# Side work of the first layer queued behind the PReLU of the iteration ahead, and two small products moved apart

## The chip, the cores and the metric

The kernel runs on one core of one Trainium2 chip. A core has five engines with an instruction queue each: TensorE (PE, matrix products; its weight loads are shown as PEld), VectorE (DVE), ScalarE (ACT), GpSimd (POOL) and SyncE (SP, which issues DMAs here). Each engine works through its own queue in order, and an instruction that waits for another engine holds up all that is behind it in its queue. The metric is the device time of one execution in microseconds (us); lower is better.

## The reference, cut to what matters

Three stages follow each other on 4608 tokens (8 batches of 576):

```python
def sm_attn(qq, kk, vv):
    s = scale * np.matmul(qq, kk.transpose(0, 1, 3, 2))
    a = np.exp(s - np.max(s, axis=-1, keepdims=True))
    return np.matmul(a / (np.sum(a, axis=-1, keepdims=True) + 1e-09), vv)
p_packed = sm_attn(p, k, v)                # 32 packed rows per head, 8 heads of 64
x = sm_attn(q, p_packed, p_packed)         # -> 4608 x 512
h = x @ w_in                               # first layer, 512 -> 2048
g = np.maximum(h, 0.0) + alpha * np.minimum(h, 0.0)     # PReLU
x = g @ w_out                              # 2048 -> 512
gate, val = x @ w_gate, x @ w_val          # second layer, 512 -> 1536
out = (gate / (1 + np.exp(-gate)) * val) @ w_out2
```

The weights come in double precision, as pairs of 32-bit words, and are narrowed on the chip; products are done in three passes (low x high, high x high, high x low) to keep float32's precision.

## The kernel before, in words

**The first layer** is a loop over 256 iterations (`it`). One iteration is one block of 128 hidden columns (`f`, 16 blocks) for one half batch of 288 tokens (`j`). `h_unit(it)` makes six products into one of two PSUM banks named `h`; then ScalarE writes `m` (alpha times h, L1003), VectorE makes the PReLU `g` from bank and `m` (L1006), ScalarE rounds it to `hi` (L1014), and GpSimd subtracts to `lo` (L1016). The bank is free for `h_unit(it + 2)` when `g` is done. `o_unit(it)` makes twelve products of `hi`, `lo` and `w_out` into the four accumulators, and stands three iterations behind `h_unit` (`LAG1 = 3`). The products with `w_in` are folded: per batch, `ppw` (`pp_win`) holds the packed attention rows times `w_in`, and `h` is made from the softmax `a2` and `ppw`.

**Beside these products** runs other work, traced in `steps(it, 0)` ahead of `h_unit(it)` and in `steps(it, 1)` behind it, so that an iteration has two slots. For batches 2 to 7 the table `STEPS` says in which slot (counted from the start of the batch ahead, 64 slots a batch) each piece of the attention of the next batch stands: loads (`k0`, `q0`, `v0`), transposes on VectorE (`kt0`, `qt0`, L614), logits (`s1a`), maximum, exponential and sums, `et0`/`et1` (transposed exponentials, L678 and L685), `pp0`/`pp1` (their products with `v`, L694, evicted at L702), `ppt`, `s2a`/`s2b`, and the second softmax (`top`, `sub`, `sum`, `mul`, `turn`, `rest`, L730 to L753). `v0` and `v1` share one buffer, so the load of `v1` waits for `pp0`. `PPW` sets the slots of `pp_win` (products L564, evictions L784 and L786). From slot 84 on (`GROUP0`) each slot also issues up to two pieces of the second layer's weight work (`more_weights2`): narrowing (`widen`, L217 to L265), differences (L927), splits into high and low (L933, L934, L944, L945) and stores to DRAM. Up to iteration 37 a table `EARLY` does the same for batches 0 and 1 and the first layer's weights (`pp_win` there evicts at L799 and L800).

**What sets the order.** The program is traced in this order, and a scheduler then lays every engine's queue by a model of the time: an instruction may stand ahead of ones traced earlier when the scheduler takes it to be ready sooner. `tc.issue_after(x)` holds it: what is traced inside the block stands behind `x` if both are on one engine. From iteration 36 on (`CHAIN0`) the products on TensorE are chained so with `behind()` and `done()`, and their queue is in the order traced. The queues of VectorE, ScalarE, GpSimd and SyncE are free, but for four conversions held by `HOLD`.

**The second layer** is a loop over 6 x 12 steps without side work from the first, apart from its own inputs (`ring` tiles, made in the last 36 iterations of the first layer by `prepare_x`).

Of the kernel before, what the change touches and what calls it, by code (L numbers as in the profile page):

```python
# [11 lines left out]
AF = mybir.ActivationFunctionType  # L12
# [60 lines left out]

STEPS = """
    8:p,k0,k1 10:pt 11:kt0,k2 12:kt1,k3,v0 14:kt2 15:kt3 17:s1a 19:s1b 20:mx0,q0,q1 21:mx1,exp0
    22:exp1 23:sums 24:et0 26:et1 28:qt0,q2,pp0,v1 29:qt1,q3 33:pp1 34:qt2 35:qt3 36:ppt 40:s2a
    42:s2b 44:top0 45:top1 46:sub0 47:sub1 49:sum0 50:sum1 51:mul0 52:mul1 53:turn0 54:turn1
    57:rest0 58:rest1
"""
# [10 lines left out]
GROUP0 = 84  # L90
# [14 lines left out]
def f32(ap):  # L105
    return ap.bitcast(F32)
# [3 lines left out]
def tile_kernel(  # L110
# [23 lines left out]
    nc = tc.nc  # L134
# [71 lines left out]
        return ap if len(other.shape) == 2 else ap.rearrange("p (c f) -> p c f", c=KC)  # L206

    raws, vals, queue, issued = [], [], [], []
    begun = {}

    def use(*cut):
        raws[:] = sum((r for r, _ in cut), [])
# [89 lines left out]
    def mm3(o, wts, xs, start, stop, **kw):  # L302
        whi, wlo = wts
        xhi, xlo = xs
        nc.tensor.matmul(o, wlo, xhi, start=start, stop=False, **kw)  # L305
        nc.tensor.matmul(o, whi, xhi, start=False, stop=False, **kw)  # L306
        return nc.tensor.matmul(o, whi, xlo, start=False, stop=stop, **kw)  # L307
# [239 lines left out]
    before, chained = [], []  # L547

    def behind():

        return tc.issue_after(before[-1].ins) if before else ExitStack()

    def done(last):
        if chained:
            before[:] = [last]
# [308 lines left out]
    plan = {}  # L864
# [14 lines left out]
    busy = set()  # L879
# [3 lines left out]
    for b in range(2, B):  # L883
        d0 = 2 * NB1 * (b - 1)
        steps_of = attention(b)
        for entry in STEPS.split():
            d, names = entry.split(":")
            slot = d0 + int(d)
# [73 lines left out]
    def more_weights2(vector):  # L962

        for _ in range(2):
            if not kinds:
                kinds.append(next(work2, None))
            if kinds[0] is None or kinds[0] == "v" and not vector:
                return
            vector = vector and kinds[0] == "p"
            kinds[:] = [next(work2, None)]  # L970
# [12 lines left out]
    def h_unit(it):  # L983
        j, f, _, _ = order[it]
        b, half = divmod(j, 2)
        w = ppw[b, f // WP]
        c = slice((f % WP) * P, (f % WP + 1) * P)
        tok = slice(half * HS, (half + 1) * HS)
        hp = ps.tile([P, 512], F32, tag="h", name=f"h{it}", bufs=2)[:, :HS]
        with behind():  # L990
            for q2 in range(NQ):
                hi, lo = a2[b, q2]
                last = mm3(
                    hp,
                    (w[:, q2, c], w[:, NQ + q2, c]),
                    (hi[:, tok], lo[:, tok]),
                    q2 == 0,
                    q2 == NQ - 1,
                )
        done(last)  # L1000
        g32 = gp.tile([P, HS], F32, tag="g32", name=f"g32_{it}", bufs=2)
        m = gp.tile([P, HS], F32, tag="r", name=f"m_{it}", bufs=2)
        begun[it] = nc.scalar.activation(  # L1003
            out=m, in_=hp, func=AF.Copy, scale=sal[:, f : f + 1]
        )
        nc.vector.scalar_tensor_tensor(  # L1006
            out=g32, in0=hp, scalar=sg[:, f : f + 1], in1=m, op0=ALU.mult, op1=ALU.max
        )
        gs[it] = split(gp, g32, it, LAG1 + 1, LAG1)

    def split(pool, x, n, bufs, bufs_lo):

        hi = pool.tile(list(x.shape), F32R, tag="hi", name=f"hi{n}", bufs=bufs)
        nc.scalar.activation(out=hi, in_=x, func=AF.Copy)  # L1014
        lo = pool.tile(list(x.shape), F32R, tag="lo", name=f"lo{n}", bufs=bufs_lo)
        nc.gpsimd.tensor_tensor(out=lo, in0=x, in1=f32(hi), op=ALU.subtract)  # L1016
        return hi, lo
# [266 lines left out]


    def steps(it, late):
        for s in plan.get((it, late), ()):
            s()
        slot = 2 * it + late
        if slot >= GROUP0:  # L1290
            more_weights2(slot not in busy)

    due = []
    for it in range(N1 + LAG1):
        if it == CHAIN0:
            chained.append(it)
        steps(it, 0)
        if it < N1:
            h_unit(it)
        steps(it, 1)  # L1300
        due.extend(range(max(it - LAG1, 0), it - LAG1 + 1))

        if it < N1 and len(due) == 1 and order[due[0]][2]:
            continue
        while due:
            o_unit(due.pop(0))
# [44 lines left out]
```

## Time and profile before

| what | value |
|---|---|
| median of 3 runs | 1750.45 us (1748.5 to 1750.59) |
| the profiled execution, its own time | 1752.87 us |
| its span, first to last instruction | 1751.1 us |
| TensorE busy | 1625.2 us (93%) |
| VectorE / ScalarE / GpSimd busy | 947.2 / 686.5 / 798.0 us |
| mean granted TensorE clock | 0.97 |

The page of the profile gives busy shares over the whole span; the stages differ, so the trace is read by stretches. A wait row tells which engine sat idle, until what, how long in total, how often, and the longest. In a timeline an idle time before an instruction stands in brackets with what ended it.

### The profile page before, as it was taken

How to read it: one execution, taken by the hardware profiler on the slowest of the kernel's cores; microseconds unless marked ns; L12 is line 12 of the kernel's file. 1: busy time of each engine (PE TensorE's matmuls, PEld its weight loads, DVE VectorE, ACT ScalarE, POOL GpSimd, SP SyncE). 2: the span in 40 equal slices, each digit the busy share in tenths (PEclk: the TensorE clock that was granted, in tenths of full speed). 3: DMA queues.
4: the chain of work that ended last, by engine and by line, in shares of the span. 5: the costliest groups of instructions: out<-in, count | busy, mean ns of one | idle time of the engine just before them, and what ended most of it. 6: DMA issues, size and time to landing. Idle time of an engine off the chain costs nothing.

```text
span 1751.1 us, 28573 instructions
## 1 busy us (share of the span) xinstructions
PE 1625.2 (93%) x10708; PEld 1468.7 (84%) x10708; DVE 947.2 (54%) x1621; ACT 686.5 (39%) x1512; POOL 798.0 (46%) x824
## 2 busy tenths in 40 slices
PE   5689789999989998999999999989999999999997
PEld 3468687878878887988999989979988998999996
DVE  6999857576675757455343363363354336335332
ACT  6775544545454454544431232232222223223221
POOL 3567755656655465423333343343333334333342
PEclk8899899999999999999999999999999999999999
DMA  9434365654555445332264464445455446445442
GB/s 227 127 98 122 114 178 153 159 151 138 151 138 152 109 139 149 79 78 81 95 245 150 166 204 163 169 163 203 169 182 185 159 148 220 167 146 186 169 169 78
DMA packets 227370, 266.11 MB, mean 152 GB/s; under 512 B 130464, under 2 KB 189856, under 8 KB 227232
## 3 DMA queue, kind: packets, MB, share of 16 engines
q1 hardware_dynamic: 227232, 264.30, 47.7%
q8 instruction: 84, 1.38, 0.3%
q14 instruction: 54, 0.44, 0.1%
HBM read 214.70 MB, written 49.55 MB: 151 GB/s over the span
## 4 chain that ended last, share of the span: by engine, by line
PE 60%; DVE 12%; DMA 9%; issue 7%; POOL 6%; ACT 3%; SPq 2%; POOLq 0%; DVEq 0%; ACTq 0%
PE o L306 5%; PE o L307 5%; PE o L305 5%; PE yb L305 4%; PE yb L307 4%; PE yb L306 4%; PE acc L1029 3%; PE acc L1030 3%; PE acc L1035 3%; DMA wgvd<-cva 3%; PE vb L306 3%; PE vb L307 3%; PE vb L305 3%; PE xb L306 3%; PE xb L307 3%
## 5 line engine op out<-in xcount | busy, mean ns | idle before, releaser
L1016 POOL TENSOR_TENSOR lo<-g,hi 128x288 fp32r<-128x288 f32 x256 | 223.8, 876 | 229.1 <-ACT hi L1014 191.8
L1223 POOL TENSOR_TENSOR s<-s,p 128x384 f32<-128x384 f32 x72 | 73.6, 1023 | 465.7 <-ACT s L1222 465.7
L1006 DVE SCALAR_TENSOR_TENSOR g<-h,sg,m 128x288 f32<-128x288 f32 x256 | 129.9, 509 | 165.8 <-ACT m L1003 145.2
L305 PE MATMUL h<-a2h,ppw 128*128 128x288 f32 x512 | 165.5, 323 | 53.8 <-DVE g L1006 46.7
L1184 DVE TENSOR_TENSOR u<-vb,u 128x384 f32<-128x384 f32 x144 | 80.2, 557 | 186.5 <-PE vb L307 186.4
L1014 ACT ACTIVATE hi<-g 128x288 fp32r<-128x288 f32 x256 | 112.7, 441 | 158.6 <-DVE g L1006 150.2
L305 PEld LDWEIGHTS h<-a2h,ppw 128*128 128x128 f32 x512 | 99.4, 194 | 89.5 <-DVE g L1006 60.8
L307 PE MATMUL o<-wp,ph 128*128 128x512 f32 x432 | 172.2, 399 | 0.0
L306 PE MATMUL o<-wp,ph 128*128 128x512 f32 x432 | 171.6, 397 | 0.0
L305 PE MATMUL o<-wp,pl 128*128 128x512 f32 x432 | 168.8, 391 | 1.6 <-POOL pl L1245 1.6
L1245 POOL TENSOR_TENSOR pl<-s,ph 128x384 fp32r<-128x384 f32 x144 | 146.7, 1039 | 28.9 <-ACT ph L1243 28.9
L307 PE MATMUL h<-a2l,ppw 128*128 128x288 f32 x512 | 154.0, 301 | 0.0
L306 PE MATMUL h<-a2h,ppw 128*128 128x288 f32 x512 | 153.9, 301 | 0.0
L305 PE MATMUL yb<-ring,gv 128*128 128x384 f32 x432 | 146.2, 338 | 6.8 <-DVE u L1184 6.6
L1003 ACT ACTIVATE m<-h,sal 128x288 f32<-128x288 f32 x256 | 125.2, 493 | 67.0 <-PE h L307 66.2
L1184 DVE TENSOR_TENSOR u<-yb,p 128x384 f32<-128x384 f32 x144 | 79.4, 551 | 132.7 <-PE yb L307 131.2
L1222 ACT ACTIVATE s<-p 128x384 f32<-128x384 f32 x72 | 37.8, 525 | 288.5 <-DVE p L1184 288.5
L307 PE MATMUL yb<-ring,gv 128*128 128x384 f32 x432 | 144.8, 335 | 0.0
L306 PE MATMUL yb<-ring,gv 128*128 128x384 f32 x432 | 144.8, 335 | 0.0
L1243 ACT ACTIVATE ph<-s 128x384 fp32r<-128x384 f32 x144 | 73.5, 524 | 150.0 <-DVE s L1227 135.3
L305 PE MATMUL xb<-ring,gv 128*128 128x384 f32 x288 | 97.8, 340 | 8.6 <-DVE u L1184 8.4
L306 PEld LDWEIGHTS h<-a2h,ppw 128*128 128x128 f32 x512 | 99.7, 195 | 0.0
(235 smaller groups left out, 4387.8 us busy)
## 6 DMA issues: line engine op xcount, KB each, us to landing
gv<-wgvd SPq DMA_DIRECT2D x144, 896.0 KB, 6.2
wgvd<-cva SPq DMA_DIRECT2D x84, 256.0 KB, 2.6
cva<-in_moe_w_out_dram SPq DMA_DIRECT2D x28, 512.0 KB, 3.7
v<-in_v_dram SPq DMA_DIRECT2D x16, 576.0 KB, 5.3
out_dram<-os SPq DMA_DIRECT2D x12, 768.0 KB, 3.7
cva<-in_moe_w_in_dram SPq DMA_DIRECT2D x16, 512.0 KB, 3.9
kr<-in_k_dram SPq DMA_DIRECT2D x96, 72.0 KB, 2.7
qr<-in_q_dram SPq DMA_DIRECT2D x96, 72.0 KB, 2.6
```

Source lines behind the costliest of these rows:

```text
L305: nc.tensor.matmul(o, wlo, xhi, start=start, stop=False, **kw)
L306: nc.tensor.matmul(o, whi, xhi, start=False, stop=False, **kw)
L307: return nc.tensor.matmul(o, whi, xlo, start=False, stop=stop, **kw)
L1003: begun[it] = nc.scalar.activation(out=m, in_=hp, func=AF.Copy, scale=sal[:, f : f + 1])
L1006: nc.vector.scalar_tensor_tensor(out=g32, in0=hp, scalar=sg[:, f : f + 1], in1=m, op0=ALU.mult, op1=ALU.max)
L1014: nc.scalar.activation(out=hi, in_=x, func=AF.Copy)
L1016: nc.gpsimd.tensor_tensor(out=lo, in0=x, in1=f32(hi), op=ALU.subtract)
L1029: nc.tensor.matmul(acc[dc], lo[:, f % WP, c], ghi, start=start, stop=False)
L1184: nc.vector.tensor_tensor(out=out, in0=bank, in1=x, op=ALU.add)
L1223: nc.gpsimd.tensor_tensor(out=s2, in0=s2, in1=p1, op=ALU.mult)
L1243: nc.scalar.activation(out=hi, in_=x, func=AF.Copy)
L1245: nc.gpsimd.tensor_tensor(out=lo, in0=x, in1=f32(hi), op=ALU.subtract)
```

## The change

Work traced in `steps` from iteration 36 on is now held behind three instructions on the same engine: the PReLU `g` of the iteration ahead (VectorE), its `m` (ScalarE), and the rounding `hi` of two iterations ahead (ScalarE). So it can no longer stand ahead of them in the queue. And in the table `pp0` (with the load `v1` behind it) moves from slot 28 to 26, `pp1` from 33 to 35, with `et1`, `qt2`, `qt3` and `ppt` by one slot each.

```diff
 STEPS = """
-    22:exp1 23:sums 24:et0 26:et1 28:qt0,q2,pp0,v1 29:qt1,q3 33:pp1 34:qt2 35:qt3 36:ppt 40:s2a
+    22:exp1 23:sums 24:et0 26:pp0,v1 27:et1 28:qt0,q2 29:qt1,q3 33:qt2 34:qt3 35:pp1 37:ppt 40:s2a
...
-    begun = {}
+    begun, made, rounded = {}, {}, {}
...
-        nc.vector.scalar_tensor_tensor(
+        made[it] = nc.vector.scalar_tensor_tensor(
             out=g32, in0=hp, scalar=sg[:, f : f + 1], in1=m, op0=ALU.mult, op1=ALU.max
         )
...
-        nc.scalar.activation(out=hi, in_=x, func=AF.Copy)
+        rounded[n] = nc.scalar.activation(out=hi, in_=x, func=AF.Copy)
...
     def steps(it, late):
-        for s in plan.get((it, late), ()):
-            s()
-        slot = 2 * it + late
-        if slot >= GROUP0:
-            more_weights2(slot not in busy)
+        with ExitStack() as held:
+            if chained:
+                for ins in made.get(it - 1), begun.get(it - 1), rounded.get(it - 2):
+                    if ins is not None:
+                        held.enter_context(tc.issue_after(ins.ins))
+            for s in plan.get((it, late), ()):
+                s()
+            slot = 2 * it + late
+            if slot >= GROUP0:
+                more_weights2(slot not in busy)
```

Three places show what this does to the queues. First VectorE at iterations 55 and 56, in the second softmax of batch 2; `g_55` and `g_56` are the PReLUs, L737 is `sum`, L743 `mul`, L748 `turn`, L786 the eviction of `ppw`. Before:

```order
L1006 SCALAR_TENSOR_TENSOR g_55_2940<-h_2933,sg,m_2941 128x288
L739 TENSOR_SCALAR sx_506<-sx_506 128x36
L740 RECIPROCAL sx_506<-sx_506 128x36
L743 TENSOR_TENSOR s2t_2_2800<-s2t_2_2800,sx_506 128x576
L743 TENSOR_TENSOR s2t_2_2801<-s2t_2_2801,sx_506 128x576
L748 STREAM_TRANSPOSE a_2_3054<-s2t_2_2800 128x576
L786 TENSOR_TENSOR ppw_0_2962<-ppw_00_2963,ppw_0_2962 128x512
L786 TENSOR_TENSOR ppw_0_2962<-ppw_01_2964,ppw_0_2962 128x512
L748 STREAM_TRANSPOSE a_2_3077<-s2t_2_2801 128x576
L1006 SCALAR_TENSOR_TENSOR g_56_2984<-h_2977,sg,m_2985 128x288
```

And the same place of VectorE's queue now:

```order
L1006 SCALAR_TENSOR_TENSOR g_55_2940<-h_2933,sg,m_2941 128x288
L737 TENSOR_REDUCE sx_506<-s2t_2_2789 128x18
L786 TENSOR_TENSOR ppw_0_2962<-ppw_00_2963,ppw_0_2962 128x512
L786 TENSOR_TENSOR ppw_0_2962<-ppw_01_2964,ppw_0_2962 128x512
L1006 SCALAR_TENSOR_TENSOR g_56_2984<-h_2977,sg,m_2985 128x288
L737 TENSOR_REDUCE sx_506<-s2t_2_2790 128x18
L739 TENSOR_SCALAR sx_506<-sx_506 128x36
L740 RECIPROCAL sx_506<-sx_506 128x36
L1006 SCALAR_TENSOR_TENSOR g_57_3015<-h_3008,sg,m_3016 128x288
L743 TENSOR_TENSOR s2t_2_2789<-s2t_2_2789,sx_506 128x576
L743 TENSOR_TENSOR s2t_2_2790<-s2t_2_2790,sx_506 128x576
L748 STREAM_TRANSPOSE a_2_3054<-s2t_2_2789 128x576
```

The eight instructions that stood between two PReLUs are spread over the iterations in which they were traced. Second, VectorE where the hold begins, between the PReLUs of iterations 36 and 37, now (L614 is a transpose of `k` for batch 2, L224 to L254 are the last two conversions of the first layer's weights, L800 evicts `ppw` of batch 1):

```order
L1006 SCALAR_TENSOR_TENSOR g_36_2092<-h_2085,sg,m_2093 128x288
L614 STREAM_TRANSPOSE kT_2_2191<-kr_2_2075 128x576
L224 TENSOR_SCALAR cva_102<-cva_102 128x512 x2
L228 TENSOR_SCALAR cva_102<-cva_102 128x512
L800 TENSOR_TENSOR ppw_2_2100<-ppw_20_2101,ppw_2_2100 128x512
L228 TENSOR_SCALAR cva_102<-cva_102 128x512
L237 SCALAR_TENSOR_TENSOR cva_102<-cva_101,cva_102 128x512
L800 TENSOR_TENSOR ppw_2_2100<-ppw_21_2106,ppw_2_2100 128x512
L237 SCALAR_TENSOR_TENSOR cva_102<-cva_101,cva_102 128x512
L246 TENSOR_SCALAR cva_101<-cva_102 128x512 x2
L800 TENSOR_TENSOR ppw_3_2111<-ppw_30_2112,ppw_3_2111 128x512
L254 SCALAR_TENSOR_TENSOR cva_101<-cva_101 128x512 x2
```

Before, those two conversions stood ahead of `g_36`, and the transposes of `k` at iterations 14 to 18; now they gather behind `g_36`. Third, the DMA queue of SyncE around the load of `v1` for batch 4 (`v_4`; `qr_4` are the loads `q2` and `q3`, `v_5` is `v0` of batch 5). Before:

```order
L597 DMA qr_4_5117<-in_q_dram 32x18x32 x4
L597 DMA qr_4_5167<-in_q_dram 32x18x32 x4
L607 DMA v_4_5148<-in_v_dram 96x4x384
L935 DMA wgvd_522<-cva_102 256x1x256
L217 DMA cva_101<-in_moe_w_gate_dram 128x4x256
L947 DMA wo2d_534<-cva_102 128x512 x2
L607 DMA v_5_6067<-in_v_dram 96x4x384
```

And now:

```order
L607 DMA v_4_5094<-in_v_dram 96x4x384
L597 DMA qr_4_5145<-in_q_dram 32x18x32 x4
L947 DMA wo2d_532<-cva_102 128x512
L597 DMA qr_4_5167<-in_q_dram 32x18x32 x3
L947 DMA wo2d_532<-cva_102 128x512
L597 DMA qr_4_5167<-in_q_dram 32x18x32
L607 DMA v_5_6067<-in_v_dram 96x4x384
```

The load of `v1` now stands ahead of those of `q2` and `q3`.

## Rows read from the trace of the kernel before

**Rows 1.** Busy time by stretch: us, busy us (count) by engine, granted clock, DMA.

```profile
core 0: us, PE busy (x) PEld busy (x) DVE busy (x) ACT busy (x) POOL busy (x), PEclk, DMA share, GB/s
134.60:205.30 70.70, 58.59 (x368) 49.65 (x370) 67.40 (x99) 39.84 (x84) 50.78 (x43) 0.90 0.42 129
...
213.20:881.50 668.30, 617.22 (x5349) 565.89 (x5349) 394.72 (x692) 332.10 (x774) 348.83 (x400) 0.97 0.47 129
881.50:1751.10 869.60, 843.93 (x4359) 778.14 (x4358) 369.02 (x615) 219.47 (x454) 323.39 (x299) 0.99 0.48 173
```

**Rows 2.** TensorE's waits from 213.2 to 881.5: total us, times, longest.

```profile
PE h L305 <- DVE g L1006: 35.1, 21, 4.8
PE pp L694 <- DMA v<-in_v_dram: 10.8, 6, 3.6
PE s L564 <- ACT E L646: 2.1, 1, 2.1
...
PE et L678 <- ACT E L658: 0.5, 1, 0.5
```

**Rows 3.** VectorE's timeline: start, us, instruction.

```profile
273.74 0.50 DVE L1006 SCALAR_TENSOR_TENSOR g<-h,sg,m 128x288 f32<-128x288 f32 x1
...
274.77 1.99 DVE L743 TENSOR_TENSOR s2t<-s2t,sx 128x576 f32<-128x576 f32 x2
276.69 0.77 DVE L748 STREAM_TRANSPOSE a<-s2t 128x576 f32<-128x576 f32 x1
277.38 1.24 DVE L786 TENSOR_TENSOR ppw<-ppw,ppw 128x512 fp32r<-128x512 f32 x2
...
279.24 0.91 DVE L1006 SCALAR_TENSOR_TENSOR g<-h,sg,m 128x288 f32<-128x288 f32 x2
```

**Rows 4.** TensorE's timeline at the same place.

```profile
276.96 0.30 PE L1029 MATMUL acc<-hi,wo3l 128*128 128x288 f32 x1
277.09 0.30 PE L1030 MATMUL acc<-hi,wo3h 128*128 128x288 f32 x1
...
279.76 0.40 PE L305 MATMUL h<-a2h,ppw 128*128 128x288 f32 x1 [1.84 <-DVE g L1006]
```

**Rows 5.** Busy time in stretches at half clock: one, ten in sum, an early one.

```profile
231.22:234.63 3.41, 3.41 (x16) 3.41 (x15) 3.34 (x6) 1.89 (x6) 1.69 (x2) 0.50 1.00 327
...
sum 40.97, PE 37.30 PEld 36.66 DVE 30.95 ACT 22.12 POOL 20.97; mean PE 3.73 PEld 3.67 DVE 3.10 ACT 2.21 POOL 2.10
...
190.26:203.91 13.65, 7.31 (x24) 5.13 (x26) 13.28 (x18) 7.09 (x16) 10.45 (x10) 0.50 0.50 161
```

**Rows 6.** SyncE's DMA queue ahead of `pp1` of batch 5; landing times of `v`.

```profile
551.18 4.39 SPq L597 DMA_DIRECT2D qr<-in_q_dram  x7
555.67 0.44 SPq L607 DMA_DIRECT2D v<-in_v_dram  x1
...
DMA to landing us min/median/max: 4.4/5.3/10.6
```

**Rows 7.** TensorE's waits from 134.6 to 213.2.

```profile
PE h L305 <- DVE g L1006: 10.9, 6, 5.0
```

**Rows 8.** `ppw` of batch 1 at iteration 36: TensorE, then VectorE.

```profile
201.58 3.07 PE L795 MATMUL ppw<-wi,ppT 128*64 128x512 f32 x8
204.98 2.18 PE L795 MATMUL ppw<-wi,ppT 128*64 128x512 f32 x8 [0.33 <-DVE ppw L800]
...
205.34 0.69 DVE L800 TENSOR_TENSOR ppw<-ppw,ppw 128x512 fp32r<-128x512 f32 x1
```

**Rows 9.** VectorE by line, 213.2 to 881.5: ns min/median/max, first and last start.

```profile
L1006 DVE SCALAR_TENSOR_TENSOR g<-h,sg,m x218: 465/516/520, 214.5 to 881.0; 128x288 f32<-128x288 f32 x109
...
L237 DVE SCALAR_TENSOR_TENSOR cva<-cva x35: 650/694/1219, 221.8 to 700.7; 128x512 uint32<-128x512 uint32 x35
```

**Rows 10.** ScalarE's waits for DMAs, 213.2 to 881.5.

```profile
ACT cva L933 <- DMA wgvd<-cva: 32.4, 29, 4.2
...
ACT cva L944 <- DMA wgvd<-cva: 15.6, 7, 4.4
```

## The prediction

> **What bounds the kernel now.** I read the busy shares by stretch first [rows 1]. From 881.5 us on, the second layer, TensorE is busy 843.9 of 869.6 us, and nothing of the change is traced there. The first layer's chained part, 213.2 to 881.5 (iterations 37 to 255), has TensorE busy 617.2 of 668.3 us, a gap of 51 us; VectorE is busy only 394.7. From 134.6 to 205.3 (iterations 15 to 36) it is the other way round: VectorE 67.4 of 70.7 us, so there it is the bound.
>
> Second, TensorE's waits in the chained part [rows 2]: 35.1 us in 21 waits of a first product of `h_unit` for a PReLU, 10.8 us in six waits of `pp` for a load of `v`, and four small groups, 2.1 down to 0.5 us and 5.0 in all. Third, one such wait from both sides [rows 3, 4]. VectorE ends a PReLU at 274.24 and then has 5.0 us of second softmax and `ppw` evictions queued before the next, which ends at 279.75; the product that needs its bank starts at 279.76 after 1.84 us of idleness. The engine is half idle on average, and late here, because work traced for iterations 57 to 59 stands ahead of the PReLU of 56. Fourth, the clock [rows 5]: ten stretches of the chained part, 41.0 us, are granted 0.50 of the clock, the lower level of 1.2 GHz. The first, from 231.2, follows a wait; all ten begin in or just behind waits that I found on TensorE's timeline. TensorE is busy 37.3 us of them.
>
> **The change part by part.** *Holding VectorE's work.* Between two PReLUs a queue can hold some work for free. Products start 0.13 us apart [rows 4], so 18 of them, an iteration, are 2.4 us; with two banks the PReLU may lag two iterations, 4.8 us, less about 1.0 for `m` and the PReLU itself: 3.8 us. I added up, from each queue's order and the median duration of each line in the trace, what VectorE does from one PReLU to the end of the next. Before, 23 of the iterations 38 to 255 exceed 3.8 us, up to 8.7, and they lie where the waits are; with the change one does, with 3.9. The largest regular ones are 3.5 us, as the pair of `mul` (1.99) with a `turn` (0.77) and the PReLU at iteration 58 [rows 3]. By that count the 35.1 us would go whole. I leave 8: a queue in order also stalls on what its instructions wait for, and a third of the later lumps lies within 0.5 us of the limit. Term: -27.1 us. Bounds: all gone (-35.1), or 20 left (-15).
>
> *Moving `pp0` and `pp1` apart.* `v1` can be issued when `pp0` is done. Before, it stood behind the seven or eight DMAs of `q2`, `q3` that take 4.4 us to issue, and landed in a median 5.3 us [rows 6]; six loads were late by 3.6 us at most [rows 2]. Now it is issued ahead of them, one iteration earlier, and `pp1` comes one iteration later: 4.8 us of room and 4.4 of queue, against 3.6. Term: 10.8 to 0.5, -10.3 (-8 at least). `pp0` now stands one iteration behind `et0`, not two; the copies between them are two ScalarE instructions, and `et1`, `pp0` may wait for them: the four small groups go from 5.0 to 6.0, +1.0 (between -5 and +4).
>
> *The clock.* At half the clock 37.3 busy us did the work of 18.7, so 18.6 us were lost. I expect four stretches out of twelve units of 3.41 us to be left, 13.7 us: loss 6.2, term -12.4 (between 0 with the waits all there, and -18.6).
>
> *Iterations 15 to 40.* Here the scheduler sees the hold only from afar. Six VectorE pieces leave the saturated stretch: transposes of `k` go from iterations 14 to 18 behind `g_36`, and the last two conversions too. The 10.9 us of waits for PReLUs [rows 7] and the 3.6 us lost in 13.65 us at half clock with TensorE busy 7.31 [rows 5] can go: -14.5. But behind `g_36` now stand 9.1 us of work ahead of `g_37`, and TensorE's third and fourth `ppw` tile wait for evictions inside it, as it did there for 0.33 us [rows 8]. By medians the first eviction ends 2.8 us behind `g_36`, which ends 1.0 behind its products; two tiles take 2.2: 1.6 us of idleness, then 0.7 more for the fourth. With instructions stretched as in that stretch I take 4 us, 2.5 more where `ppw` of iterations 27 and 28 now meets another lump, and 3 us for clock. -14.5 + 9.5 = -5.0 (bounds -14.5 and +5).
>
> *End of the first layer.* The weight work was pulled ahead before and ended near 701 us [rows 9]; now it ends about iteration 251. The `ring` tiles that reuse its staging buffers, for the third, fourth and fifth product of the second layer, are then made at iterations 253 and 254, behind the landing of the last store. There are two iterations and three `o_unit`s of cover, 9 us: +1 (0 to +5). If that cover is gone, ScalarE's `m` of 253 waits behind the ring copy.
>
> The Sigmoid table's load goes from the program's start to iteration 247, and one at the second layer's start goes away; both lie beside busy products: 0.
>
> **Sum**, against the profiled execution's own 1752.87 us (span 1751.1): -27.1 - 10.3 + 1.0 - 12.4 - 5.0 + 1.0 = -52.8, so 1700.1. The median of the runs stands 2.4 us below that execution: **1698 us**. With all best bounds the sum is -84.0 (1666), with all worst ones -9 (1741).
>
> **The rivals.**
>
> *The waits move to ScalarE and the attention.* Held pieces come later, and in the chained part TensorE reads them at fixed places (`s1`, `et`, `pp`, `ppt`, `s2`, four `ppw` in six batches, some 70 places). If half of the gain by PReLUs and clock comes back so, 20 us and some clock, the time is 1722. For it: such waits exist, with 2.1 us once [rows 2]. Against it: they are 5.0 us in all, and the table leaves an iteration or more between steps.
>
> *VectorE's instructions stretch.* A weight step on VectorE such as L237 runs from 650 to 1219 ns, 694 at the median, while the PReLU never leaves 465 to 520 [rows 9]. In the saturated stretch GpSimd was busy 50.8 of 70.7 us [rows 1]. With the hold a weight step stands in front of most PReLUs; 36 chains of five with 0.8 us of stretch each, all on the path, are 29 us: 1727. Against it: they are spread, and lumps with a chain and no slack are few. The Trainium skill, "SBUF — State Buffer", section "Who interferes with whom", says that a VectorE instruction with two inputs in SBUF, or in a two-port mode, is blocked wholly by a GpSimd one that holds the shared ports, and that one with a single SBUF input outside these modes is not. This trace agrees: the PReLU reads one tensor from SBUF and is never stretched, L237 reads two. By that rule this rival's 29 us are lost, as every weight step may have to wait out a GpSimd instruction.
>
> *ScalarE blocks on DMAs, and the kernel is slower.* ScalarE sat idle 48.0 us until stores of the staging buffers landed [rows 10], free as long as this ran ahead. Now each such instruction is tied to an iteration, between two `m`; a late landing stops `m`, the PReLU and TensorE. If all 48.0 us, and the half-rate clock behind some 36 waits at up to 1.7 us each (61), came on the path, the gain of 52.8 would be lost twice; it is slower from half of these 109 us on. With two thirds, 73 us: 1771. Against it: the hold ties instructions behind an iteration, it does not pull them forward, and the buffers alternate as before.
>
> *Little happens.* The waits are late for other reasons than the work queued ahead (a product or `m` that is late itself), and only `pp` gains, 10.3 us and 4 of clock: 1736. Against it rows 3: VectorE has no idle time in that lump.
>
> **How the numbers follow.** Forecast 60%, moved waits 13%, stretched steps 11%, little 8%, slower 8%. What can be told from no change is about 0.2%, 3.5 us: the first four are all faster, but for 3% of the "little" case at its edge. So faster 0.89, same 0.03, slower 0.08. The forecast's own bounds are 1666 to 1741; the range to be right 8 times in 10 is 1676 to 1738, leaving out the slower case and the best tail.
>
> **What would show it.** Waits of `h` for the PReLU in the chained part under 12 us in under ten waits; no wait of `pp` for `v` over 1 us; under 20 us of half clock from 213 on; the chained part some 48 us shorter, 620 us; VectorE's lumps between PReLUs under 4 us; a wait of 2 to 5 us near the `ppw` of iteration 36; the second layer as long as before, 869.6 us within 3. It is wrong if the PReLU waits stay above 20 us (then the lumps were not their cause), or if waits for `m` or for attention copies take their place, or if ScalarE's waits for DMAs grow and stand before late `m`s.

## The result, and the profile after

The changed kernel takes 1726.47 us at the median (1723.2 to 1727.06), beside 1749.47 us for the kernel before on the same chip: a ratio of 0.9867, 95% interval 0.9849 to 0.9884. It is faster by 23 us. The forecast was 1698; the time lies inside the stated range, 28 us above the forecast, and the gain is 23 us where 53 were forecast. The profiled execution spans 1723.9 us, 27.2 less than before. The views below show where they come from.

Busy time by stretch (columns as in [rows 1]): from the PReLU of iteration 37 to that of 255, and the rest. The first is 23.6 us shorter than before (644.7 for 668.3), where 48 were forecast; the second layer's 867.6 stand for 869.6.

```profile
211.60:856.30 644.70, 611.23 (x5360) 557.90 (x5359) 387.16 (x700) 331.03 (x777) 353.53 (x402) 0.98 0.50 134
856.30:1723.90 867.60, 842.85 (x4353) 775.79 (x4352) 371.28 (x615) 217.93 (x453) 323.57 (x299) 0.99 0.49 174
```

TensorE's waits in the first of them (total us, times, longest), the answer to [rows 2]. The PReLU waits fell from 35.1 to 14.4, and the waits of `pp` for `v` are gone. But where other waits were 5.0 us in all, they are 18.9 now: `s` waits for transposes of `k`, and `pp`, `ppt` and `et` wait for copies of ScalarE.

```profile
PE h L305 <- DVE g L1006: 14.4, 12, 2.6
PE s L564 <- DVE kT L614: 6.4, 2, 3.2
PE pp L694 <- ACT ET L685: 3.7, 4, 2.0
PE ppt L626 <- ACT ppbd L702: 2.8, 1, 2.8
PE et L678 <- ACT ppbd L702: 2.7, 4, 1.2
PE s L564 <- DVE s2t L721: 1.6, 2, 1.0
PE acc L1029 <- ACT x1s L1051: 1.4, 2, 1.0
```

Five stretches at half the clock [rows 5 has ten], one and the sum:

```profile
599.99:606.82 6.83, 6.25 (x37) 4.75 (x38) 2.86 (x5) 1.78 (x5) 3.81 (x5) 0.50 0.55 111
...
sum 20.47, PE 18.53 PEld 15.80 DVE 14.03 ACT 8.85 POOL 10.55; mean PE 3.71 PEld 3.16 DVE 2.81 ACT 1.77 POOL 2.11
```

ScalarE's waits for DMAs in the chained part, the answer to [rows 10]. L933 and L944 wait for stores of prepared weights, 59.6 us, where before they waited 48.0. L222, the first step on a loaded piece of second-layer weights, waits 42.7 us for loads.

```profile
ACT cva L933 <- DMA wgvd<-cva: 49.1, 38, 4.3
ACT cva L222 <- DMA cva<-in_moe_w_val_dram: 26.7, 12, 4.2
ACT cva L222 <- DMA cva<-in_moe_w_gate_dram: 13.8, 7, 3.2
ACT cva L944 <- DMA wgvd<-cva: 10.5, 5, 3.7
ACT cva L222 <- DMA cva<-in_moe_w_out_dram: 2.2, 1, 2.2
```

The same rows of the kernel before, which I had not read for the prediction, 18.2 us for loads:

```profile
ACT cva L222 <- DMA cva<-in_moe_w_val_dram: 17.8, 11, 3.2
...
ACT cva L222 <- DMA cva<-in_moe_w_gate_dram: 0.4, 1, 0.4
```

Two of the waits, followed through the engines' timelines (start, us, instruction, idle time before it in brackets). The first is a plain case. ScalarE's L222 waits 3.46 us for its load, `m` stands behind L222, the PReLU behind `m`, and TensorE's `h` waits 2.64 us for the PReLU:

```profile
294.87 0.66 ACT L222 ACTIVATE cva<-cva 128x512 f32<-128x512 f32 x1 [3.46 <-DMA cva<-in_moe_w_val_dram]
295.43 0.49 ACT L1003 ACTIVATE m<-h,sal 128x288 f32<-128x288 f32 x1
```

```profile
296.02 0.52 DVE L1006 SCALAR_TENSOR_TENSOR g<-h,sg,m 128x288 f32<-128x288 f32 x1
```

```profile
296.60 0.61 PE L305 MATMUL h<-a2h,ppw 128*128 128x288 f32 x1 [2.64 <-DVE g L1006]
```

The second has two causes at once. GpSimd frees the buffer, and SyncE issues the load of `w_val` at once. ScalarE's L222 stands next in its queue and waits 4.15 us. VectorE's L224 waits for L222, and the transpose of `k` behind it starts at 599.75. TensorE's `s` waits 3.19 us, until 600.58, and the granted clock falls to half within this wait, at 599.99. But the last three pieces of `k`, issued from 592.09 to 593.41 behind the same load, took 5.3 to 5.9 us to land, the last at 598.66: without the block on ScalarE the transpose could have come 1.1 us earlier, not more.

```profile
590.28 1.32 POOL L265 TENSOR_TENSOR cva<-cva 128x512 f32<-128x512 f32 x1 [0.63 <-DVE cva L254]
```

```profile
591.63 0.42 SPq L217 DMA_DIRECT2D cva<-in_moe_w_val_dram  x1
```

```profile
597.83 0.66 ACT L222 ACTIVATE cva<-cva 128x512 f32<-128x512 f32 x1 [4.15 <-DMA cva<-in_moe_w_val_dram]
598.40 0.48 ACT L1003 ACTIVATE m<-h,sal 128x288 f32<-128x288 f32 x1
```

```profile
598.52 0.43 DVE L224 TENSOR_SCALAR cva<-cva 128x512 f32<-128x512 f32 x1 [4.64 <-ACT cva L222]
598.98 0.52 DVE L1006 SCALAR_TENSOR_TENSOR g<-h,sg,m 128x288 f32<-128x288 f32 x1
599.42 0.41 DVE L228 TENSOR_SCALAR cva<-cva 128x512 uint32<-128x512 uint32 x1
599.75 0.77 DVE L614 STREAM_TRANSPOSE kT<-kr 128x576 f32<-128x576 f32 x1
```

```profile
600.58 0.69 PE L564 MATMUL s<-kT,pT 64*32 64x288 f32 x2 [3.19 <-DVE kT L614]
```

The other wait of `s`, 3.18 us until 699.37, has no wait of ScalarE for a DMA in the 6.5 us before it. There VectorE itself waits for `k`:

```profile
698.53 0.78 DVE L614 STREAM_TRANSPOSE kT<-kr 128x576 f32<-128x576 f32 x1 [2.99 <-DMA kr<-in_k_dram]
```

So there is a second way in which the DMAs of the weight work can act: some loads of `k` land late. Their time from issue to landing in the chained part is shown below (us, minimum, median, maximum). The maximum was 4.2 before, and is 4.5 in e4 below, without the weight loads:

```profile
DMA to landing us min/median/max: 2.3/2.8/5.9
```

I went through all of TensorE's waits of this part. Ahead of 20 of the 28 (26.1 of 33.2 us), ScalarE had waited at least 1 us for DMAs in the 6.5 us before their end; in the kernel before of 11 out of 32 (14.1 of 50.9 us). A moment taken at random in this part has such a wait behind it in 38% of the cases, in the kernel before in 24%: the tie is clear, but this count alone does not show the cause. The gain also has a shape in time. From iteration 37 to 152 the stretch went from 380.1 to 341.7 us, a lead of 38 us; from 152 to 255 it went from 288.3 to 303.0 and gave 15 back. There TensorE's waits grew from 14.7 to 17.8 us, and the time at half clock from 6.6 to 13.7. Of its 35 weight steps L237 the kernel before had 8 left at iteration 152, the last at 700.7 [rows 9]; the changed kernel has 16 of its 36, the last at 831.8, and each piece stands between two PReLUs.

### The profile page after: what moved, and what is told of

Same layout as the page of the kernel before. It is cut to its first block, busy times and chain, and to the rows that moved or that the text cites. A ratio compares the mean times of both kernels' runs of the same rounds, so it can differ in the third digit from the quotient of the medians.

```text
span 1723.9 us, 28559 instructions
## 1 busy us (share of the span) xinstructions
PE 1623.3 (94%) x10708; PEld 1462.9 (85%) x10708; DVE 928.5 (54%) x1621; ACT 682.7 (40%) x1511; POOL 801.2 (46%) x824
## 4 chain that ended last, share of the span: by engine, by line
PE 68%; DMA 9%; DVE 8%; issue 5%; POOL 4%; ACT 4%; SPq 2%; POOLq 0%; ACTq 0%; DVEq 0%
PE o L306 5%; PE o L307 5%; PE o L305 5%; PE acc L1029 5%; PE acc L1030 4%; PE acc L1035 4%; PE yb L305 4%; PE yb L307 4%; PE yb L306 4%; DMA wgvd<-cva 4%; PE vb L306 3%; PE vb L307 3%; PE vb L305 3%; PE h L305 3%; PE xb L306 3%
## 5 line engine op out<-in xcount | busy, mean ns | idle before, releaser
L1016 POOL TENSOR_TENSOR lo<-g,hi 128x288 fp32r<-128x288 f32 x256 | 227.3, 889 | 237.7 <-ACT hi L1014 195.1
L305 PE MATMUL h<-a2h,ppw 128*128 128x288 f32 x512 | 163.0, 318 | 22.7 <-DVE g L1006 16.9
L306 PE MATMUL h<-a2h,ppw 128*128 128x288 f32 x512 | 152.8, 298 | 0.0
L305 PEld LDWEIGHTS h<-a2h,ppw 128*128 128x128 f32 x512 | 98.2, 192 | 56.9 <-DVE g L1006 27.1
L1003 ACT ACTIVATE m<-h,sal 128x288 f32<-128x288 f32 x256 | 125.5, 492 | 42.1 <-PE h L307 41.0
L307 PEld LDWEIGHTS h<-a2l,ppw 128*128 128x128 f32 x512 | 98.1, 192 | 0.8 <-issue 0.8
```

The source lines that it names most:

```text
L1003: begun[it] = nc.scalar.activation(out=m, in_=hp, func=AF.Copy, scale=sal[:, f : f + 1])
```

## The experiments

**Theory A:** ScalarE blocks until DMAs of the weight work land, and the hold places these blocks between an `m` and the next, where the PReLU, the transposes and the copies stand behind them. **Theory B:** it is the amount of weight work that now lies late. **Theory C:** it is the traffic and the queue's issues, which delay the loads of `k`, `q` and `v`, not ScalarE's waits. Ratios are to the kernel before on the same chip, with the 95% interval. The other columns are from one profiled execution of each kernel, in us: the chained part (PReLU 37 to 255), TensorE's waits for the PReLU and all its waits in it, and ScalarE's waits for weight loads and stores.

| kernel | ratio | part | PReLU | all | loads | stores |
|---|---|---|---|---|---|---|
| before | 1 | 668.3 | 35.1 | 50.9 | 18.2 | 48.0 |
| changed | 0.9867 (0.9849 to 0.9884) | 644.7 | 14.4 | 33.3 | 42.7 | 59.6 |
| e1 table only | 0.9982 (0.9969 to 0.9994) | 670.2 | 41.2 | 51.9 | 23.0 | 42.3 |
| e2 hold only | 0.9900 (0.9885 to 0.9914) | 652.1 | 13.3 | 37.7 | 37.2 | 54.1 |
| e3 weights free | 0.9969 (0.9955 to 0.9983) | 668.0 | 35.3 | 50.3 | 31.1 | 45.7 |
| e8 VectorE's hold only | 0.9854 (0.9840 to 0.9869) | 647.3 | 14.6 | 32.3 | 42.1 | 43.0 |
| e10 hold to 151 | 0.9916 (0.9890 to 0.9942) | 657.7 | 30.6 | 42.5 | 30.9 | 52.9 |
| e4 no loads | 0.9635 (0.9621 to 0.9649) | 609.9 | 5.5 | 10.9 | 2.0 | 46.8 |
| e9 loads turned | 0.9704 (0.9679 to 0.9730) | 617.8 | 9.0 | 17.4 | 1.7 | 50.6 |
| e13 no stores | 0.9654 (0.9632 to 0.9676) | 616.1 | 10.9 | 16.5 | 44.7 | 6.8 |
| e14 neither | 0.9562 (0.9544 to 0.9579) | 603.0 | 7.1 | 8.0 | 2.6 | 6.6 |
| e12 before, no loads | 0.9940 (0.9920 to 0.9960) | 657.6 | 27.9 | 41.8 | 1.4 | 51.3 |
| e7 prefetch, no hold | 0.9965 (0.9953 to 0.9978) | 661.9 | 36.5 | 47.4 | 6.8 | 51.2 |
| e6 prefetch | 0.9762 (0.9747 to 0.9776) | 627.6 | 9.3 | 23.9 | 6.5 | 46.3 |
| e11 prefetch, paced | 0.9758 (0.9725 to 0.9791) | 623.7 | 13.5 | 19.7 | 4.9 | 49.6 |

### The parts of the change: e1, e2, e8

e1 is the kernel before with the new line of the table:

```diff
-    22:exp1 23:sums 24:et0 26:et1 28:qt0,q2,pp0,v1 29:qt1,q3 33:pp1 34:qt2 35:qt3 36:ppt 40:s2a
+    22:exp1 23:sums 24:et0 26:pp0,v1 27:et1 28:qt0,q2 29:qt1,q3 33:qt2 34:qt3 35:pp1 37:ppt 40:s2a
```

> The kernel before with the changed table alone (pp0 and v1 earlier, pp1 and ppt later), without the hold. If the waits of pp for v were the whole effect of the table, the 10.8 us of them go, with some 2 to 4 us of half clock behind them: about 1736 us, and the waits for the PReLU stay at 30 to 40 us. If pp0 one iteration behind et0 costs the attention (copies ET and ppbd late), 4 us or more come back there: 1741 to 1745 us.

Neither case came out. It gained 0.2%, not the 13 to 15 us of the additive case, and the chained part gained nothing (670.2 us for 668.3). The waits of `pp` for `v` are gone, but the PReLU waits are 41.2 us where they were 35.1, and all waits together 51.9 where they were 50.9. What TensorE no longer lost at `pp` it lost at late PReLUs and at copies of ScalarE.

e2 is the changed kernel with the old table, the same line the other way round:

> The changed kernel with the old table: the hold alone. If hold and table add up, the waits for the PReLU are about 14 us as in the changed kernel, the waits of pp for v about 10 us, and the time is 1736 to 1738 us. If the table costs something in the late iterations (152 to 255) of the changed kernel, this one is no slower than the changed kernel there (152 to 255: under 303 us) and ends at or below 1730 us.

The PReLU waits fell as in the changed kernel, 13.3 us, and the waits for `v` stayed (14.6). The hold alone gives 1.0%, and the table 0.3% on top of it. Iterations 152 to 255 took 303.4 us, as in the changed kernel, so the table is not what cost there.

e8 keeps one of the three pins:

```diff
-                for ins in made.get(it - 1), begun.get(it - 1), rounded.get(it - 2):
+                for ins in (made.get(it - 1),):
```

> The changed kernel with the hold behind the PReLU on VectorE alone, not behind the two instructions of ScalarE. If VectorE's order is what the hold mends, the time is that of the changed kernel within 5 us (about 1731 on this chip). If ScalarE's order carries part of it, waits for the PReLU with an m that is late come back, 5 us or more: 1737 us or above. If the pins on ScalarE are what ties the loads' waits to the path, it is faster: 1722 us or below.

The same as the changed kernel, within the intervals: the pins on ScalarE do nothing that can be told, for good or ill; VectorE's order is what the hold mends.

### Where the hold acts: e3, e10

e3 issues the weight work outside the hold:

```diff
             for s in plan.get((it, late), ()):
                 s()
-            slot = 2 * it + late
-            if slot >= GROUP0:
-                more_weights2(slot not in busy)
+        slot = 2 * it + late
+        if slot >= GROUP0:
+            more_weights2(slot not in busy)
```

> The changed kernel, but the work on the second layer's weights is issued outside the hold; attention and ppw stay held. Theory A and B (what was given back after iteration 152 is the weight work that is now tied to late iterations): iterations 152 to 255 take about 288 us as in the kernel before, against 303 in the changed one, and the time is about 1712 us unless early iterations lose. Rival (the weight steps were the lumps ahead of the PReLUs): waits for the PReLU return to 25 us or more and the time is 1735 us or above.

Both halves came true, and they cancel: iterations 152 to 255 took 290.9 us, but 37 to 152 took 377.1, nearly as long as before. The PReLU waits are back at 35.3 us. So it is the hold on the weight steps that gains.

e10 drops the hold late:

```diff
-            if chained:
+            if chained and it < 152:
```

> The changed kernel with the hold only up to iteration 151. If what is given back after iteration 152 comes from holding the weight work there, iterations 152 to 255 take 288 us as in the kernel before and the time is 1714 to 1718 us. If the loads cost the changed kernel wherever the hold acts, and lumps cost where it does not, the two cancel: 152 to 255 takes 298 us or more and the time is 1724 us or above.

Iterations 152 to 255 took 306.1 us, more than with the hold. Letting go where the gain was given back does not bring it back: the lumps return. But iterations 37 to 152, held as in the changed kernel, took 351.6 us instead of 341.7, with about the same waits (16.3 us for 15.5) and 13.9 us at half clock instead of 6.8. So the scheduler did not leave the early part as it was, and the run does not show the late hold by itself.

### The waits for DMAs: e4, e5, e9, e13, e14, e12

e4 leaves out all but the first three loads:

```diff
-        issued.append(nc.sync.dma_start(out=like(raw, src), in_=src))
+        if raw is not spots.get("raw") or len(issued) < len(ORDER.split()) + 3:
+            issued.append(nc.sync.dma_start(out=like(raw, src), in_=src))
```

> The changed kernel with all but the first three of the 36 loads of second-layer weights left out (VectorE, ScalarE and GpSimd work on what the buffer holds, so the second layer's weights are not the given ones). Theory A (ScalarE blocks for the landing of a weight piece, 42.7 us in 20 waits, and the rounding, the copy m and the transposes of k stand behind it): the waits of TensorE near iterations 168, 177 and 242 go, iterations 152 to 255 take 290 us or less, the time is 1710 to 1716 us. Theory B (the sheer amount of weight work in late iterations): 1722 us or above, and the late waits stay.

More than theory A said: 34.8 us less in the chained part than the changed kernel, over the whole of it (323.7 us to iteration 152, 286.2 behind). Theory B fell: the amount of work is the same. TensorE's waits in e4:

```profile
PE h L307 <- DVE g L1007: 5.5, 4, 2.1
PE et L680 <- ACT ppbd L704: 3.1, 4, 1.6
PE pp L696 <- ACT ET L687: 1.0, 1, 1.0
PE s L566 <- DVE kT L616: 0.9, 1, 0.9
```

e5 was to keep the traffic and drop the wait, by copies in DRAM:

```diff
+        else:
+            scrap = dram.tile([P, 1024], U32, name=f"scrap{next(scraps)}")
+            nc.sync.dma_start(out=like(scrap, src), in_=src)
```

> As e4, but each left-out load is replaced by a copy of the same 512 KB from the weights to a place in DRAM that nothing reads, at the same place in the program: the queue's issues and the traffic stay, only nobody waits for them. Theory A (what costs is ScalarE's wait for the landing): within 5 us of e4, 1690 to 1697 us. Theory C (what costs is the loads' traffic and their issues on the queue, which delay k, q and v): well above it, 1715 us or more, with waits of s for k transposes back.

Inconclusive. The copies wait for nothing, and all 33 were issued between 16 and 81 us (the hold binds only instructions of one engine, and behind VectorE's and ScalarE's SyncE is not held), where they held up the start: the PReLU of iteration 36 ended at 237.7 instead of 199.1. The ratio was 0.9876 (0.9857 to 0.9894); the chained part, then free of loads and their traffic, took 610.0 us like e4's.

e9 does it in place, beside e4's lines, with a store out of the buffer for each load left out:

```diff
+        else:
+            scrap = dram.tile([P, 1024], U32, name=f"scrap{next(scraps)}")
+            nc.sync.dma_start(out=scrap, in_=raw)
```

> As e4, but each left-out load is replaced in its place by a store of the same 512 KB out of the same buffer into a place in DRAM that nothing reads: it waits for the same work of GpSimd as the load did and keeps the queue's issues, the traffic and what stands behind them; only ScalarE does not wait for it (VectorE overwrites the buffer some microseconds later). Theory A (the wait for the landing costs): the chained part takes 608 to 616 us (609.9 in e4, 644.7 in the changed kernel), the time is 1688 to 1698 us. Theory C (traffic and issues cost): 630 us or more there, 1712 us or above.

617.8 us, just above theory A's bounds, far from C's. The stretch had the changed kernel's DMA share, 0.50:

```profile
211.00:828.80 617.80, 600.32 (x5344) 551.73 (x5345) 390.80 (x700) 336.60 (x778) 356.08 (x402) 0.99 0.50 140
```

Of the 34.8 us that the loads cost, 26.9 go when each load becomes a store that nobody waits for, and 7.9 stay. Not all of the 26.9 need be ScalarE's wait: such a store holds up the loads of `k` less than a load does (4.5 us to landing at most in e9, 5.9 in the changed kernel), and the waits of `s` for transposes of `k` fell with it, from 6.4 to 1.9 us. I estimate that part at 10 us at most: these 4.5 us, and some 5 for the two stretches of half clock at those waits (half of 6.83 and 3.41). So theory A carries most of the 26.9, and how much falls to the delay of `k`, a part of theory C, is left open.

I now took the waits for stores to cost nothing, since e9 keeps 50.6 us of them. e13 leaves out the stores instead (from the second piece on), e14 both loads and stores, by e4's edit and this one:

```diff
-        nc.sync.dma_start(
-            out=wgvd[f][:, :, k, :], in_=f32(stage).rearrange("p (t n) -> p t n", t=2)
-        )
+        if f == 0:
+            nc.sync.dma_start(
+                out=wgvd[f][:, :, k, :], in_=f32(stage).rearrange("p (t n) -> p t n", t=2)
+            )
...
-        for t in range(2):
-            nc.sync.dma_start(out=wo2d[f][:, t, :], in_=f32(stage[t]))
+        if f < 2:
+            for t in range(2):
+                nc.sync.dma_start(out=wo2d[f][:, t, :], in_=f32(stage[t]))
...
-            nc.sync.dma_start(out=f32(gvw[n][t]), in_=wgvd[f][:, t])
+            nc.sync.dma_start(out=f32(gvw[n][t]), in_=wgvd[0][:, t])
...
-            nc.sync.dma_start(out=f32(w[:, e]), in_=wo2d[2 * i + e])
+            nc.sync.dma_start(out=f32(w[:, e]), in_=wo2d[e])
```

> The changed kernel with its loads, but the stores of the prepared second-layer weights left out from the second piece on (the second layer reads the first piece's, so its result is not the given one). ScalarE waited 59.6 us for these stores and 42.7 us for loads in the changed kernel. If only the loads cost (in e9, with 50.6 us of waits for stores left, TensorE waits 17.4 us): chained part 640 us or more, 1722 us or above. If both kinds of wait cost alike, by their length: 25 us or more of the chained part go, 1702 us or below.

> Loads left out as in e4 and stores as in e13. If the waits for stores cost nothing beside those for loads: within 4 us of e4 in the chained part (609.9), about 1688 us. If they are what is left of the waits (10.9 us in e4): 602 us or less and 1682 us or below.

That idea fell in e13: 28.6 us went from the chained part with the stores, while the waits for loads stayed at 44.7 us:

```profile
ACT cva L222 <- DMA cva<-in_moe_w_val_dram: 26.8, 12, 3.7
ACT cva L222 <- DMA cva<-in_moe_w_gate_dram: 17.6, 10, 2.8
ACT cva L933 <- DMA wgvd<-cva: 6.8, 4, 3.1
```

Each kind of DMA costs some 29 to 35 us beside the other, but both together only 41.7 (644.7 to 603.0): the second to go brings 6.9 or 13.1. A reading that fits is that an iteration has room for one block of a few microseconds and not for two; it was not tested by itself. e13 also takes the stores' traffic and issues away, and no run does that for stores apart from the wait. e14's 603.0 lies between its two cases: the stores cost 6.9 us beside absent loads.

e12 leaves the loads out of the kernel before, by e4's edit:

> The kernel before, without hold and with the old table, with all but the first three loads of second-layer weights left out (the second layer's weights are not the given ones). If the loads cost only where the hold ties them to an iteration (theory A): 1741 us or above, waits for the PReLU stay above 25 us. If they cost the kernel before as much as the changed one (34.8 us of its chained part): 1720 us or below.

10.7 us of its chained part, at the edge of the first case: the same loads cost 0.6% there and 2.3% in the changed kernel (0.9635 for 0.9867). It is the hold that makes these loads dear (the changed table goes with it here; by e1 it gains the chained part nothing alone). Read the other way: with the loads left out of both kernels, the change takes the chained part from 657.6 to 609.9 us. That is 47.7 us, close to the 48 that were forecast, though the stores still cost in both; with the loads in, it is 23.6.

### A kernel that keeps everything: e6, e7, e11

In e6 `w_gate` is loaded into the scratch tiles of the products, `w_val` and `w_out` into the old buffer, each as soon as its buffer is free (`fetch` is the load alone, `widen` no longer issues it):

```diff
...
         weights2()
+        fetch(w_gate, "g", 0)
+        fetch(w_val, "v", 0)
         for f in range(NF2):
             yield from columns2(w_gate, "g", f)
             yield from columns2(w_val, "v", f)
+            fetch(w_out2, "o", f)
             for i in range(len(PRODUCTS)):
                 yield from product2(f, i)
+                if i == 5 and f + 1 < NF2:
+                    fetch(w_gate, "g", f + 1)
...
         yield from widen(w_out2[f * P : (f + 1) * P, :], raw, val, loaded=True)
+        if f + 1 < NF2:
+            fetch(w_val, "v", f + 1)
```

> The changed kernel with every load issued ahead: w_gate goes into the four scratch tiles of the products, w_val and w_out into the old buffer, each load as soon as its buffer is free, six steps or more before its first reader. Nothing is left out. Theory A: ScalarE's waits for loads fall from 42.7 us to under 10, the waits of TensorE in the chained part to about 15 us (14.1 in e4), the time is 1688 to 1700 us, and this is the best kernel. If the loads are slowed by their own traffic (theory C) or wait for the scratch tiles: 1710 us or more.

1708.31 us, a gain of 2.4% on the kernel before and about 1% on the changed one, though short of the 1700. The waits for loads fell to 6.5 us, TensorE's to 23.9. What is left is of the same kind. Of the three largest waits, 5.85 us until 685.17 and 4.24 us until 326.09 stand behind loads of `w_gate` and `w_val`, and 3.82 us until 574.29 behind a store. In the largest, the last piece of `k` also landed late, at 683.62, 0.7 us before its transpose began:

```profile
572.28 0.63 ACT L958 ACTIVATE cva<-cva 128x512 fp32r<-128x512 f32 x1 [3.80 <-DMA wgvd<-cva]
...
682.42 0.66 ACT L223 ACTIVATE cva<-cva 128x512 f32<-128x512 f32 x1 [3.31 <-DMA cva<-in_moe_w_gate_dram]
```

This is the advice of the Trainium skill, "DMA: Bandwidth & Descriptors", section "Rules for kernel authors": issue the DMA early, compute, and wait for it late. The runs agree, with 17.1 us of the chained part (644.7 to 627.6).

e7 is the same without the hold:

> The same prefetch and the changed table, without the hold. Theory A says that the hold and the prefetch are separate: without the hold the lumps ahead of the PReLUs stay, 25 us or more of waits for the PReLU, 1730 us or above. Rival (the waits for loads were the lumps from the start, and the hold does little once they are gone): within 8 us of e6.

The lumps stay (36.5 us of PReLU waits), and the gain is 0.35%: the prefetch pays through the hold, as e12 said.

e11 adds a pace to e6: a product ends its slot, the products run in the order 0, 2, 1, 3, 4, 5, 6, and from the third on each is followed by one VectorE step of `w_out`; `GROUP0` is 80:

```diff
-        yield "p"
+        yield "q"
...
+            if last:
+                return
```

> e6 (hold, table, loads issued ahead) with the weight work paced: at most one product with its store in a slot, the VectorE steps of w_out between the products, begun two iterations earlier. Theory A: the waits of ScalarE for stores and for the late w_gate loads that stood ahead of the last waits of TensorE in e6 (3.8 us near 574, 5.9 us near 685) go, the waits in the chained part fall from 27.4 to about 15 us and the time to 1692 to 1702 us. If pacing only moves them: within 4 us of e6's 1708.

1708.07 us, the same as e6, and not the 1692 to 1702 of theory A: pacing only moved the waits, from the attention (13.4 to 6.2 us) to the PReLU (9.3 to 13.5).

## Why the prediction was right or wrong

**The direction and the two mechanisms were right.** The PReLU waits fell because VectorE's lumps went: by VectorE's busy time in the trace, from the end of one PReLU to the end of the next, 22 of the iterations 38 to 255 had more than 3.8 us before (the prediction counted 23 by medians), and one has now. No `pp` waits for `v` any more; `v` lands in 4.1 to 7.2 us (4.4 to 10.6 in [rows 6]), now with room ahead of its reader. The wait of 2 to 5 us at `ppw` near iteration 36 came [rows 8]:

```profile
201.39 3.68 PE L795 MATMUL ppw<-wi,ppT 128*64 128x512 f32 x8 [3.04 <-DVE ppw L800]
```

**The step that failed** is the one that gave the DMAs of the weight work no price in the sum: ScalarE's waits for them above all, and the loads of `k` that land late beside them. It is in three terms. The prediction left "8" of the PReLU waits for what a queue in order stalls on: 14.4 stayed, so the term was -20.7 for -27.1. It let the small groups go "from 5.0 to 6.0": they came to 18.9, so +13.9 for +1.0, far outside the bounds of -5 and +4 (the other two terms stayed inside theirs). And of the half clock "four stretches out of twelve units" became six units in five stretches. Four of these have a wait of ScalarE for a DMA shortly ahead of them; the one at 698.97 falls in the wait for a late `k`. With 18.53 us busy in 20.47 the loss is 9.3 us, so the term was -9.3 for -12.4. Together these are 22.4 us of the 25.6 by which the span's gain falls short of the sum (27.2 for 52.8). With loads and stores out of the way (e14) the PReLU waits are 7.1 us, the small groups 0.9, the half clock 6.8 and the chained part 603.0. So the hold does what the three terms said, and more, when these DMAs are gone; e14 takes their traffic away with ScalarE's waits.

**The other terms.** `pp` and `v`: -10.8 for -10.3. Iterations 15 to 40: the PReLU of 37 ends 1.6 us earlier (211.6 for 213.2), for -5.0. The PReLU waits of [rows 7] are nearly gone, but three waits took their place, two of them not foreseen (TensorE's waits from 130 to 211.6):

```profile
PE acc L1035 <- POOL lo L1016: 3.0, 1, 3.0
PE ppw L795 <- DVE ppw L800: 3.0, 1, 3.0
PE acc L1029 <- DVE x1s L1049: 2.7, 1, 2.7
PE h L305 <- DVE g L1006: 1.8, 3, 0.9
```

And three stretches there still lie at half clock, in sum:

```profile
sum 13.65, PE 12.89 PEld 7.37 DVE 11.89 ACT 5.09 POOL 7.12; mean PE 4.30 PEld 2.46 DVE 3.96 ACT 1.70 POOL 2.37
```

TensorE is busy for nearly all of them, so 6.4 us are lost, where 3.6 were before and the prediction took 3.

The end of the first layer showed no cost. The terms as measured sum to -20.7 - 10.8 + 13.9 - 9.3 = -26.9 in the chained part, where the time fell by 23.6. The other 3.3 us lie in TensorE's busy time, which fell by 6.0 us (617.2 to 611.2) and not by the 9.3 of the clock; why is open. With -1.6 and the second layer's -2.0 that is the span's -27.2.

**The rivals.** "ScalarE blocks on DMAs" had the mechanism: ScalarE's waits for DMAs grew from 66 to 102 us and stood before late work, as its signs of being wrong had said. But I set it beside the forecast, as an outcome of its own in which the kernel is slower, instead of a cost inside the sum. I took its waits from the stores alone [rows 10], and its price as all or two thirds of the waits. In truth 41.7 us of the chained part hang on those DMAs in the changed kernel (e14), and the change gains all the same. "The waits move to ScalarE and the attention" described the outcome best: 1722 us, at 13%, with 13.9 us of new waits in the small groups. I argued against it from the slots between the steps of the table. They are no room when both engines that fill them stand behind one DMA.

"VectorE's instructions stretch" fell, though its time, 1727, is the one that was measured: that is luck. The stretch is there. Over the 36 chains the five steps L224, L228, L237, L246 and L254 together take 20.6 us more than by their medians (L237 5.0 of it, 36 times 831 less 693 ns), where 29 were named. But before the change it was 25.7 us, and in e14, where the chained part is 603.0, it is 29.8: the change did not bring it, and it is not what holds up the PReLUs. First the line's minimum, median and maximum, then its group with count, busy us and mean; last L246:

```profile
L237 DVE SCALAR_TENSOR_TENSOR cva<-cva x36: 671/693/1324, 228.4 to 831.8; 128x512 uint32<-128x512 uint32 x36
```

```profile
L237 DVE SCALAR_TENSOR_TENSOR cva<-cva 128x512 uint32<-128x512 uint32 x36 | 29.9, 831 | 0.4
```

```profile
L246 DVE TENSOR_SCALAR cva<-cva x36: 382/428/1076, 229.4 to 832.6; 128x512 uint32<-128x512 uint32 x36
```

The Trainium skill ("SBUF — State Buffer", section "Who interferes with whom") names two kinds of VectorE instructions that a GpSimd instruction can block: those with two SBUF inputs, and those in a two-port mode. The trace agrees in that L237 has two such inputs and goes up to 1324 ns, while the PReLU has one and never takes more than 520. L246 has one as well and reaches 1076; whether it runs in a two-port mode no run here shows. "Little happens" was wrong: the hold alone gives 1.0%.

## What to carry to other kernels

When work is pinned to fixed places between the steps of a critical loop, every wait that it used to hide by running ahead is pinned with it: before pricing the pin, list all DMA waits of each engine in that work, loads as well as stores, and see what stands behind each in the queue, also on the engine that waits for the waiting one, and which other loads land late beside them. Give such work its data ahead of its place (e6), or the pin gives back part of its gain. And when several stalls share the same slack, the gains of removing them do not add: measure the pair.

## What the runs showed that I had not expected

Taking away either the loads or the stores of the same work gave 34.8 or 28.6 us of the chained part, both together 41.7. The table, worth 10.8 us of waits by the trace, gave 3 us alone, none of it in the chained part, and about 6 beside the hold. And half clock did not fall evenly with the waits: e9, e13 and e14, with 8.0 to 17.4 us of waits, have 6.8 us of it each from the PReLU of 37 on, while e6 with 23.9 has as much as the changed kernel with 33.3, 20.5 us. e4, with 10.9, has one stretch, at 1.2 GHz, with TensorE busy throughout; it begins 1.5 us after a wait of 1.96 us:

```profile
791.11:794.52 3.41, 3.41 (x16) 3.41 (x15) 3.38 (x8) 2.09 (x6) 2.32 (x3) 0.50 1.02 300
```
